# A retention and gated-MLP kernel on one core: the first heads' keys and values loaded unconverted and cast on three engines

## The chip, the cores and the metric

The kernel runs on one core of a Trainium2 chip. The metric is the device time of one launch in microseconds (us), the median of several runs. The engines of the core work side by side: TensorE (matmuls, PE in the profile, its weight loads PEld), VectorE (DVE), ScalarE (ACT), GpSimd (POOL) and SyncE (SP). Transfers are issued by SP, ACT and GpSimd and carried out by 16 DMA engines that all of them share. In the profile the loads that GpSimd issues are the queue q0, "software_dynamic"; those of SP and ACT are q1 and q10, "hardware_dynamic".

## The reference

Two layers follow each other, all in float32:

```python
# q, k, v: (8 batches, 8 heads, 576 positions, 64)
scores = q @ k.T / sqrt(64)
gamma  = 1 - 2 ** (-5 - head)
D      = gamma ** (i - j) where i >= j, else 0        # i query, j key position
ret    = (scores * D) @ v                             # (8, 8, 576, 64)
x      = ret with the heads side by side              # (4608, 512)
h      = x @ w_in                                     # (4608, 2048)
g      = h * clip(h + 3, 0, 6) / 6
out    = g @ w_out                                    # (4608, 512)
```

The inputs are q, k and v of 9.4 MB each and two weights of 4.2 MB each.

## The kernel before

**Tiles.** The 576 positions of a batch are cut into a head of 64 and a rest of 512. The heads of all eight batches together are one block of 512 tokens (block 0); the rests are blocks 1 to 8. Block 0 has a special path, in which the eight attention heads are taken in four pairs i = 0 to 3. The rests are worked in 36 chunks of 128 positions, with a running state between chunks. A block's result xT (512 features by 512 tokens) goes into the first product in 16 units ("up" units), each of eight matmuls that accumulate in PSUM, followed by one operation on ACT (u, L514) and one on DVE (g, L516), and then into the second product. From block 2 on that is a Strassen scheme with sums of weights and of g.

**Order.** Everything stands under a manual schedule: the order in which the program names operations is the order on each engine, and a queue that waits holds everything behind it on that engine. A hand-written plan (strings and tables) orders all that comes after block 0's first units. The changed lines lie ahead of this plan, in the first 25 us.

**Block 0 in the old order (L752 to L822).** `indices` and `make_identity` make small tables. Keys and q of pair 0 are loaded in float32 by SP and ACT (`load_half`, L403, one load for each head of the pair, 128 partitions of 1 KB); q of the other pairs follow on the same two queues. On GpSimd's queue come the keys of pairs 1 to 3 (six loads), the values of all pairs (eight loads, `load_values`, L443), the four pieces of w_in (`win_piece`, L679, the first in two halves) and the four of w_out (`wout_piece`, L684). All loads of this queue convert from float32 to float16 on the way. Loads with `keys` as last argument wait until the first keys have landed. Between the first two key loads and the rest GpSimd sets `pick` to zero (L767), a table of 128 x 2048 float16 that `picks` later fills with four strided copies of `by_chunk`.

`distances` (L107 to L113, on DVE) makes the table of i - j, with a huge number where j > i; `mask_of_heads(i)` (L118, on ACT) makes exp(log(gamma) x distance) for the two heads of a pair. For each pair, `cast_heads` makes float16 of keys or q (L416), `turn_heads` transposes them by eight small matmuls and a copy out of PSUM (L423, L428, L430), `scores_heads` forms the scores and multiplies them by the mask on DVE (L471, L474), `values_heads` brings the values into the order of the keys by 32 matmuls with `pick` and a copy (L454, L455), and `inner_heads` multiplies scores and values and copies the result into xT (L483, L485). `idle_products(n)` are matmuls whose result is not used. The first four up units are interleaved, one quarter of the accumulation at a time, because quarter i needs only the result of pair i.

Behind the up units, `decays` (16 small operations on GpSimd and one on ACT) makes the powers that the chunks need, `mask_of_chunk` and `decays_of_chunk` the mask and the powers of a chunk (GpSimd, L133 to L138 and L130). `fetch(8, wout[0])` lets SP load the first chunks, and waits for the first piece of w_out to land, so that these loads don't compete with the weights.

PSUM has six buffers of one kind (`pp`: scores, inner products, up units) and two of another (`st`: transposes and values).

```python
        if nm not in hd.setdefault(i, {}):
            if queue is nc.gpsimd:
                hd[i][nm] = heads16(i, nm)
```

These lines of `load_half` give GpSimd's loads a float16 target, and with it the conversion.

Of the kernel before, what the change touches and what calls it, by code (L numbers as in the profile page):

```python
# [21 lines left out]
def kernel(  # L22
# [9 lines left out]
    nc = tc.nc  # L32
# [356 lines left out]
    def after(i, behind):  # L389
        tc.add_manual_dep(i.ins, behind.ins.name,  # L390
                          mybir.DependencyInfo(mybir.DependencyClass.Sync, mybir.DependencyReason.SCHED_ONLY),
                          reason="goes first")

    def load_half(i, nm, e, queue, behind=None):

        if nm not in hd.setdefault(i, {}):
            if queue is nc.gpsimd:
                hd[i][nm] = heads16(i, nm)
            else:
                f = half_tile(io, "fq", i, FP32, "hq", bufs=2) if nm == "q" else io.tile(  # L400
                    [P, H * D], FP32, tag=f"f{nm}", name=f"h{nm}{i}")
                hd[i][nm] = f.rearrange("p (e j d) -> p e j d", e=2, j=NJ)
        d = queue.dma_start(hd[i][nm][:, e].rearrange("p j d -> p (j d)"),  # L403
                            dict(q=q, k=k, v=v)[nm][:, 2 * i + e, 0:TL, :].rearrange("b (r j) d -> r b (j d)", j=NJ))
        if behind is not None:
            after(d, behind)
        return d

    def heads16(i, nm):
        if nm == "q":  # L410
            return half_tile(work, "q16", i, FP16, "hq16_", bufs=2).rearrange("p (e j d) -> p e j d", e=2, j=NJ)
        return work.tile([P, 2, NJ, D], FP16, tag=f"{nm}16", bufs=dict(k=4, v=NV16)[nm], name=f"h{nm}16_{i}")
# [22 lines left out]
    def picks():  # L435
        for j in range(NJ):
            nc.vector.tensor_copy(pick[:, j].rearrange("p c (x j) -> p (c x) j", j=NJ)[:, :, j], by_chunk)

    def load_values(i, behind=None):

        t = heads16(i, "v")
        for e in range(2):
            d = nc.gpsimd.dma_start(t[:, e].rearrange("p j d -> p (j d)"),  # L443
                                    v[:, 2 * i + e, 0:TL, :].rearrange("b (r j) d -> r b (j d)", j=NJ))
            if behind is not None:
                after(d, behind)
        hd.setdefault(i, {})["v"] = t

    def values_heads(i, copy):

# [224 lines left out]
    def win_piece(n, parts=1, behind=None):  # L675
        a, b = pieces_in[n]
        for i in range(parts):
            cc = slice(NP // parts * i, NP // parts * (i + 1))
            d = nc.gpsimd.dma_start(win16[n][:, cc], win_v[:, cc, BLK * a:BLK * b])  # L679
            if behind is not None:  # L680
                after(d, behind)

    def wout_piece(pc):
        return nc.gpsimd.dma_start(wout16[:, JQ * pc:JQ * pc + JQ, :], wout_v[pc])  # L684
# [63 lines left out]

    with tc.manual_schedule(engines={ENG.PE, ENG.DVE, ENG.Pool, ENG.Activation, ENG.SP}):
        sp, act, pool = nc.sync, nc.scalar, nc.gpsimd  # L750
        on_act, on_dve = nc.scalar.copy, nc.vector.tensor_copy
        indices()  # L752
        for nm in ("k", "q"):
            landed = load_half(0, nm, 0, sp)
            keys = landed if nm == "k" else keys
            load_half(0, nm, 1, act)
        nc.scalar.activation(warm, half, ACTF.Exp)
        load_half(1, "q", 0, sp)
        load_half(1, "q", 1, act)
        for i in (2, 3):  # L760
            for e in range(2):
                load_half(i, "q", e, sp, keys)
        for i in (1, 2, 3):
            for e in range(2):
                load_half(i, "k", e, pool, None if i == 1 else keys)
            if i == 1:
                nc.gpsimd.memset(pick, 0.0)  # L767
        for i in range(NP):
            load_values(i)
        win_piece(0, 2)  # L770
        for n in (1, 2, 3):
            win_piece(n)
        wout = [wout_piece(pc) for pc in (0, 2, 1, 3)]
        distances()
        idle_products(5)
        mask_of_heads(0)
        cast_heads(0, "k", on_dve)
        picks()
        turn_heads(0, "k", on_act)
        mask_of_heads(1)  # L780
        idle_products(4)
        cast_heads(0, "q", on_dve)
        mask_of_heads(2)
        turn_heads(0, "q", on_act)
        cast_heads(1, "q", on_dve)
        turn_heads(1, "k", on_act)
        turn_heads(1, "q", on_act)
        cast_heads(2, "q", on_dve)
        scores_heads(0)
        mask_of_heads(3)  # L790
        idle_products(1)
        turn_heads(2, "k", on_act)
        turn_heads(2, "q", on_act)
        cast_heads(3, "q", on_dve)
        scores_heads(1)
        idle_products(1)
        turn_heads(3, "k", on_act)
        turn_heads(3, "q", on_act)
        scores_heads(2)
        values_heads(0, on_act)  # L800
        scores_heads(3)
        values_heads(1, on_act)
        inner_heads(0, on_act)
        values_heads(2, on_dve)
        inner_heads(1, on_dve)
        values_heads(3, on_act)
        inner_heads(2, on_dve)
        first = [up_steps(0, u) for u in range(4)]
        for dmc in range(3):
            for unit in first:  # L810
                next(unit)
            if dmc == 1:
                inner_heads(3, on_act)
        for unit in first:
            for _ in unit:
                pass
        decays()
        mask_of_chunk()
        decays_of_chunk()
        fetch(8, wout[0])  # L820
        for u in range(4, NFC):
            up_unit(0, u)  # L822
        weight_sums(3)
# [74 lines left out]
```

## Time and profile before

| What | Value |
|---|---|
| Median of three runs | 299.42 us (298.52 to 299.57) |
| The profiled execution | 301.09 us, its span 299.4 us |
| Granted TensorE clock | 1.00 |
| Loaded through GpSimd's queue | 4720 packets, 5.11 MB written |
| Read from HBM, written to it | 36.70 MB, 9.44 MB |

The span runs from the first to the last recorded instruction; the execution's own time is 1.7 us longer. "Busy" counts work of an engine and not its waits. In a timeline each line has the start in the span, the length (of all the instructions that were merged into it), the engine, the line of the kernel, the operation with what it writes and reads, and how often; in brackets stands the idle time ahead of it and what ended it. A DMA instruction on an engine's line is only the issue; the transfer comes later.

### The profile page before, as it was taken

To read this page: it belongs to the slowest core of one execution; us is meant where nothing else is said; L and a number is where in the kernel's file an instruction comes from. 1 tells how busy PE (TensorE), PEld (TensorE's weight loads), DVE (VectorE), ACT (ScalarE), POOL (GpSimd) and SP (SyncE) were. 2 spreads that over 40 slices of the span, in tenths; PEclk is the share of its full clock that TensorE was granted. 3 is DMA by queue.
4 is the path that set the end of the run, shared out by engine and by line. 5 is a ranking of instruction groups with operands and counts; after the bars stand their busy time and mean duration, and the time that the engine had idled before them with its cause. 6 is when DMAs were issued, how large, how long until landed. Compare 5 with 4: busy or idle time off the path is not lost.

```text
span 299.4 us, 12624 instructions
## 1 busy us (share of the span) xinstructions
PE 287.2 (96%) x5574; PEld 219.8 (73%) x5574; DVE 216.0 (72%) x380; ACT 190.5 (64%) x343; POOL 133.9 (45%) x169
## 2 busy tenths in 40 slices
PE   4998999999999999999989999999999999999995
PEld 2675655877556667898768878988787787778894
DVE  8648768859835678788957796678759776647654
ACT  3738855778866687585767577667766574565420
POOL 8961046656841912529621962296237003100510
PEclk9999999999999999999999999999999999999999
DMA  7999989996999999999999899989908100200114
GB/s 164 148 182 214 231 204 228 242 243 120 186 209 168 246 197 221 172 202 205 239 219 212 147 201 215 151 162 259 141 11 145 73 2 29 102 15 2 72 72 140
DMA packets 119542, 47.86 MB, mean 160 GB/s; under 512 B 92352, under 2 KB 114880, under 8 KB 119488
## 3 DMA queue, kind: packets, MB, share of 16 engines
q1 hardware_dynamic: 114336, 41.56, 71.3%
q0 software_dynamic: 4720, 5.11, 10.6%
q8 instruction: 43, 0.70, 1.0%
q10 hardware_dynamic: 432, 0.39, 0.5%
q14 instruction: 11, 0.09, 0.1%
HBM read 36.70 MB, written 9.44 MB: 154 GB/s over the span
## 4 chain that ended last, share of the span: by engine, by line
PE 77%; DMA 10%; POOL 6%; ACT 3%; DVE 2%; issue 1%; SPq 0%; POOLq 0%; ACTq 0%
PE ph L153 36%; PE pm L153 29%; DMA wout<-in_moe_w_out_dram 5%; PE pd L153 4%; PE po L232 3%; DMA fq<-in_q_dram 3%; PE pa L232 2%; DMA fv<-in_v_dram 2%; POOL hv L443 1%; POOL hk L403 1%; POOL win L679 1%; PE pu L232 1%; POOL q L192 1%; ACT z L327 1%; ACT kT L211 1%
## 5 line engine op out<-in xcount | busy, mean ns | idle before, releaser
L153 PE MATMUL ph<-xT,win 128*64 128x512 f16 (+1 forms) x1248 | 144.5, 364 | 1.5 <-DMA win<-in_moe_w_in_dram 1.5
L516 DVE SCALAR_TENSOR_TENSOR g<-u,ph 128x512 f16<-128x512 f32 x132 | 89.6, 684 | 50.4 <-ACT u L514 49.9
L514 ACT ACTIVATE u<-ph,half 128x512 f32<-128x512 f32 x132 | 90.3, 691 | 42.6 <-PE ph L153 40.1
L153 PEld LDWEIGHTS <-win 128*64 128x64 f16 x1248 | 83.1, 136 | 28.4 <-DMA win<-in_moe_w_in_dram 2.1
L153 PEld LDWEIGHTS <-g 128*64 128x64 f16 x928 | 50.6, 110 | 15.5 <-issue 0.4
L153 PEld LDWEIGHTS <-s 128*64 128x64 f16 x896 | 51.0, 110 | 8.2 <-issue 1.1
L321 POOL TENSOR_TENSOR z<-z,gpow 128x256 f32<-128x256 f32 x24 | 16.2, 673 | 67.5 <-DVE z L320 44.8
L153 PE MATMUL pm<-ws,s 128*64 128x256 f16 x672 | 46.1, 273 | 0.2 <-issue 0.2
L192 POOL TENSOR_TENSOR q<-fq,dec 128x512 f16<-128x512 f32 x30 | 35.6, 1204 | 17.2 <-DMA fq<-in_q_dram 17.2
L195 POOL TENSOR_TENSOR v<-fv,dec 128x512 f16<-128x512 f32 x32 | 36.2, 1134 | 2.6 <-PE ph L153 2.6
L612 POOL TENSOR_TENSOR u<-u,p 128x512 f32<-128x512 f32 x7 | 8.9, 1271 | 62.0 <-ACT u L652 55.8
L373 ACT CAST xT<-po 128x256 f16<-128x256 f32 (+1 forms) x44 | 22.6, 585 | 21.4 <-PE po L232 21.4
L153 PE MATMUL pd<-wout,g 128*64 128x512 f16 x256 | 34.2, 382 | 0.1
L153 PE MATMUL pm<-wout,g 128*64 128x256 f16 x448 | 30.8, 273 | 0.0
L267 DVE TENSOR_TENSOR a<-pa,mask 128x256 f16<-128x256 f32 (+1 forms) x44 | 21.9, 539 | 10.3 <-PE pa L232 6.9
L548 DVE TENSOR_TENSOR s<-g 128x1024 f16<-128x1024 f16 x28 | 19.4, 694 | 0.2
L327 ACT CAST z<-z 128x512 f16<-128x512 f32 x24 | 14.9, 620 | 7.0 <-DVE z L317 6.6
L188 ACT CAST k<-fk 128x512 f16<-128x512 f32 x29 | 18.0, 621 | 1.0 <-DMA fk<-in_k_dram 1.0
L153 PE MATMUL pm<-ws,g 128*64 128x256 f16 x224 | 16.9, 274 | 0.0
L153 PE MATMUL pm<-wout,s 128*64 128x256 f16 x224 | 16.7, 273 | 0.2
L232 PE MATMUL po<-qT,z 64*64 64x64 f16 x512 | 12.6, 198 | 1.3 <-ACT z L327 0.7
L232 PEld LDWEIGHTS <-z 64*64 64x64 f16 x512 | 8.0, 106 | 7.5 <-ACT z L327 2.5
(111 smaller groups left out, 292.6 us busy)
## 6 DMA issues: line engine op xcount, KB each, us to landing
fk<-in_k_dram SPq DMA_DIRECT2D x32, 256.0 KB, 4.7
fq<-in_q_dram SPq DMA_DIRECT2D x16, 512.0 KB, 6.0
fv<-in_v_dram SPq DMA_DIRECT2D x32, 256.0 KB, 5.7
out_dram<-o SPq DMA_DIRECT2D x14, 512.0 KB, 3.6
wout<-in_moe_w_out_dram POOLq DMA_DIRECT2D x4, 512.0 KB, 18.9
out_dram<-o SPq DMA_DIRECT2D x7, 256.0 KB, 5.7
win<-in_moe_w_in_dram POOLq DMA_DIRECT2D x3, 512.0 KB, 12.5
hq<-in_q_dram SPq DMA_DIRECT2D x6, 128.0 KB, 4.7
```

Of the source, the lines that this page charges most:

```text
L153: nc.tensor.matmul(out[r], lhs[:, r], rhs, skip_group_check=True, **flags)
L188: (nc.gpsimd.tensor_copy if c in K_POOL else nc.scalar.copy)(by_head(k16), in_rows(st[c]["fk"]))
L192: (nc.vector if e and c in Q_DVE else nc.gpsimd).tensor_tensor(by_head(q16[:, e]), in_rows(st[c]["fq"][:, :, e, :]), in_rows(dd[:, 2 + e, ...
L195: nc.gpsimd.tensor_tensor(v16, st[c]["fv"], dd[:, 1, H:2 * H, :], ALU.mult)
L232: return lambda: nc.tensor.matmul(*args, skip_group_check=True, **flags)
L267: nc.vector.tensor_tensor(a16[:, a, 0:n].rearrange("p x i q -> p (x i) q"), pa[a].rearrange("p x i q -> p (x i) q"), m, ALU.mult)
L321: nc.gpsimd.tensor_tensor(new, new, decay, ALU.mult)
L327: nc.scalar.copy(z16, zs[c])
L373: nc.scalar.copy(xt[:, s], po[s].rearrange("p x n (e r) -> p x n e r", e=2))
L514: nc.scalar.activation(uu[:, 0:n], ph[:, 0:n], ACTF.Relu, bias=half, scale=1.0 / 6.0)
L516: nc.vector.scalar_tensor_tensor(out=g[:, hf, ths, jr, :], in0=by_half(uu), scalar=1.0, in1=by_half(ph), op0=ALU.min, op1=ALU.mult)
L548: nc.vector.tensor_tensor(*pend.popleft())
```

## The change

- Keys and values of block 0 that GpSimd loads come as float32 into float32 tiles, on the same queue, and are cast on the way to their use: keys of pairs 1 to 3 on DVE, values of pair 0 on ACT, values of pairs 1 to 3 on GpSimd. `load_values` goes.
- `distances` and all four `mask_of_heads` come ahead of the rest of the heads' work.
- `mask_of_chunk` and `decays_of_chunk` move from behind the up units to GpSimd's place between the keys of pair 1 and the other loads, where the memset of `pick` was. That memset goes to DVE.
- GpSimd's loads come in another order (values 0, keys 2, keys 3, values 1 to 3), then pieces 0 and 1 of w_in, then GpSimd's three casts, then pieces 2 and 3 and w_out.
- The first scores come ahead of the transposes of pair 1's q; `picks` comes after them; values of pair 0 are worked before the scores of pair 2, and the first inner product before the scores of pair 3. Two copies move from DVE to ACT. Three idle products stand where four were.

```diff
-            if queue is nc.gpsimd:
-                hd[i][nm] = heads16(i, nm)
-            else:
-                f = half_tile(io, "fq", i, FP32, "hq", bufs=2) if nm == "q" else io.tile(
-                    [P, H * D], FP32, tag=f"f{nm}", name=f"h{nm}{i}")
-                hd[i][nm] = f.rearrange("p (e j d) -> p e j d", e=2, j=NJ)
+            f = half_tile(io, "fq", i, FP32, "hq", bufs=2) if nm == "q" else io.tile(
+                [P, H * D], FP32, tag=f"f{nm}", name=f"h{nm}{i}")
+            hd[i][nm] = f.rearrange("p (e j d) -> p e j d", e=2, j=NJ)
...
-        for i in (1, 2, 3):
+        distances()
+        for i in range(NP):
+            mask_of_heads(i)
+        for e in range(2):
+            load_half(1, "k", e, pool)
+        mask_of_chunk()
+        decays_of_chunk()
+        for i, nm in ((0, "v"), (2, "k"), (3, "k"), (1, "v"), (2, "v"), (3, "v")):
             for e in range(2):
-                load_half(i, "k", e, pool, None if i == 1 else keys)
-            if i == 1:
-                nc.gpsimd.memset(pick, 0.0)
-        for i in range(NP):
-            load_values(i)
+                load_half(i, nm, e, pool, keys)
         win_piece(0, 2)
-        for n in (1, 2, 3):
-            win_piece(n)
-        wout = [wout_piece(pc) for pc in (0, 2, 1, 3)]
-        distances()
+        win_piece(1)
         idle_products(5)
-        mask_of_heads(0)
         cast_heads(0, "k", on_dve)
-        picks()
+        nc.vector.memset(pick, 0.0)
         turn_heads(0, "k", on_act)
-        mask_of_heads(1)
-        idle_products(4)
+        idle_products(3)
         cast_heads(0, "q", on_dve)
-        mask_of_heads(2)
         turn_heads(0, "q", on_act)
-        cast_heads(1, "q", on_dve)
+        cast_heads(1, "k", on_dve)
         turn_heads(1, "k", on_act)
+        cast_heads(1, "q", on_dve)
+        scores_heads(0)
+        idle_products(1)
         turn_heads(1, "q", on_act)
+        picks()
+        cast_heads(0, "v", on_act)
+        cast_heads(2, "k", on_dve)
         cast_heads(2, "q", on_dve)
-        scores_heads(0)
-        mask_of_heads(3)
-        idle_products(1)
+        scores_heads(1)
         turn_heads(2, "k", on_act)
         turn_heads(2, "q", on_act)
+        idle_products(1)
+        values_heads(0, on_act)
+        cast_heads(3, "k", on_dve)
         cast_heads(3, "q", on_dve)
-        scores_heads(1)
+        scores_heads(2)
         idle_products(1)
         turn_heads(3, "k", on_act)
         turn_heads(3, "q", on_act)
-        scores_heads(2)
-        values_heads(0, on_act)
+        for i in (1, 2, 3):
+            cast_heads(i, "v", on_pool)
+        for n in (2, 3):
+            win_piece(n)
+        wout = [wout_piece(pc) for pc in (0, 2, 1, 3)]
+        inner_heads(0, on_act)
+        values_heads(1, on_act)
         scores_heads(3)
-        values_heads(1, on_act)
-        inner_heads(0, on_act)
-        values_heads(2, on_dve)
-        inner_heads(1, on_dve)
+        values_heads(2, on_act)
+        inner_heads(1, on_act)
         values_heads(3, on_act)
         inner_heads(2, on_dve)
...
         decays()
-        mask_of_chunk()
-        decays_of_chunk()
         fetch(8, wout[0])
```

More of the change, by code (lines that the diff above doesn't have):

```diff
@@ L437, in picks @@
             nc.vector.tensor_copy(pick[:, j].rearrange("p c (x j) -> p (c x) j", j=NJ)[:, :, j], by_chunk)
[L439 to L447, printed above, removed]
     def values_heads(i, copy):
@@ L750 @@
         sp, act, pool = nc.sync, nc.scalar, nc.gpsimd
-        on_act, on_dve = nc.scalar.copy, nc.vector.tensor_copy
+        on_act, on_dve, on_pool = nc.scalar.copy, nc.vector.tensor_copy, nc.gpsimd.tensor_copy
         indices()
@@ L762 @@
                 load_half(i, "q", e, sp, keys)
-        for i in (1, 2, 3):
-            for e in range(2):
-                load_half(i, "k", e, pool, None if i == 1 else keys)
-            if i == 1:
-                nc.gpsimd.memset(pick, 0.0)
-        for i in range(NP):
-            load_values(i)
+        distances()
[6 more added lines that the diff above has]
+        for i, nm in ((0, "v"), (2, "k"), (3, "k"), (1, "v"), (2, "v"), (3, "v")):
+            for e in range(2):
+                load_half(i, nm, e, pool, keys)
         win_piece(0, 2)
-        for n in (1, 2, 3):
-            win_piece(n)
-        wout = [wout_piece(pc) for pc in (0, 2, 1, 3)]
-        distances()
+        win_piece(1)
         idle_products(5)
-        mask_of_heads(0)
         cast_heads(0, "k", on_dve)
-        picks()
-        turn_heads(0, "k", on_act)
-        mask_of_heads(1)
-        idle_products(4)
-        cast_heads(0, "q", on_dve)
-        mask_of_heads(2)
-        turn_heads(0, "q", on_act)
-        cast_heads(1, "q", on_dve)
-        turn_heads(1, "k", on_act)
-        turn_heads(1, "q", on_act)
+        nc.vector.memset(pick, 0.0)
+        turn_heads(0, "k", on_act)
+        idle_products(3)
+        cast_heads(0, "q", on_dve)
+        turn_heads(0, "q", on_act)
+        cast_heads(1, "k", on_dve)
+        turn_heads(1, "k", on_act)
+        cast_heads(1, "q", on_dve)
+        scores_heads(0)
+        idle_products(1)
+        turn_heads(1, "q", on_act)
+        picks()
+        cast_heads(0, "v", on_act)
+        cast_heads(2, "k", on_dve)
         cast_heads(2, "q", on_dve)
-        scores_heads(0)
-        mask_of_heads(3)
-        idle_products(1)
+        scores_heads(1)
         turn_heads(2, "k", on_act)
         turn_heads(2, "q", on_act)
+        idle_products(1)
+        values_heads(0, on_act)
+        cast_heads(3, "k", on_dve)
         cast_heads(3, "q", on_dve)
-        scores_heads(1)
+        scores_heads(2)
         idle_products(1)
```

## The prediction

> **What bounds the kernel now.** I read the page's busy shares first, then the chain that ended last, then the waits of TensorE, then the first 45 us engine by engine, because the change touches nothing behind that. On the page TensorE is busy nearly all the time:
>
> ```profile
> PE 287.2 (96%) x5574; PEld 219.8 (73%) x5574; DVE 216.0 (72%) x380; ACT 190.5 (64%) x343; POOL 133.9 (45%) x169
> ```
>
> so only its start and its gaps can move. The chain in order of time (start, length, what) shows that the start isn't TensorE's own:
>
> ```profile
> 3.05 1.81 POOL ws L767
> 4.86 2.57 POOL hk L403 x4
> 7.43 3.10 POOL hv L443 x6
> 10.55 1.04 POOL hv L443 x2
> 11.59 3.61 POOL win L679 x5
> 15.20 15.97 DMA wout<-in_moe_w_out_dram
> ...
> 31.80 9.42 DMA fq<-in_q_dram
> ...
> 41.39 1.46 POOL q L192
> ...
> 42.89 0.64 PE ptq L153 x16
> ```
>
> GpSimd issues one long stream of loads, the DMA engines work it off, the first piece of wout lands at 31.17, the loads of the chunks are held back for it, and TensorE meets that chain at 42.89. The waits of TensorE from 16 to 45 us say how near its own work is:
>
> ```profile
> PE ph L153 <- DMA win<-in_moe_w_in_dram: 1.5, 2, 1.0
> PE ptq L153 <- POOL q L192: 0.2, 1, 0.2
> ```
>
> and its timeline where they are:
>
> ```profile
> 17.89 0.39 PE L483 MATMUL hpo<-ha,ws 128*64 128x128 f16 x8
> 18.77 1.95 PE L153 MATMUL ph<-xT,win 128*64 128x512 f16 x16 [0.49 <-DMA win<-in_moe_w_in_dram]
> ...
> 23.68 10.58 PE L153 MATMUL ph<-xT,win 128*64 128x512 f16 x96 [0.98 <-DMA win<-in_moe_w_in_dram]
> ```
>
> At 18.77 it waits for the first half of w_in's piece 0, at 23.68 for piece 1; from there it has no gap of 0.1 us until 42.89. So two things set the end: when piece 1 lands, and when wout's first piece lands. Both are the GpSimd stream. The heads' work on the other engines only has to be done by 22.7.
>
> **The stream itself.** Is it held by issue or by the DMA engines? The queues in the windows 7 to 9 and 9 to 11 us (packets, MB, share of the 16 engines):
>
> ```profile
> q0 software_dynamic: 337, 0.16, 60.9%
> q1 hardware_dynamic: 345, 0.31, 57.5%
> ...
> q0 software_dynamic: 634, 0.29, 118.3%
> ```
>
> Shares add to over 100%: the engines are full. A packet of the converting queue costs 1.183 x 16 x 2 us / 634 = 60 ns, one of the unconverted q loads 0.575 x 32 / 345 = 53 ns, though the first writes 512 B and the second 1 KB. Both read 1 KB. The packet records give medians of 60 and 47 ns for these, and 98 and 324 ns for converting packets that read 2 and 8 KB: a slope by bytes read, plus some 22 ns on GpSimd's queue against 9 on the others. Even the 4-byte completion packets take 22 against 9. I read the 13 ns as a cost of that queue, not of converting.
>
> **The change, part by part.**
> - Loads without conversion: 14 loads of 128 packets stay 14 loads of 128 packets that read 1 KB. Between 0 and 13 ns saved on 1792 packets, over 16 engines: 0 to 1.46 us of full DMA time; if the wider write costs anything, below nothing, which full-rate 1 KB writes on the other queue at 47 ns make unlikely. I take 0.
> - GpSimd before the stream: the memset of pick (1.84 us) goes; the mask and powers come (from 22.78 to 24.14 in the trace: 1.36). The stream starts 0.4 to 0.5 us earlier, at about 4.4; keys of pair 0 must have landed, which they had by 4.76 at the latest.
> - Twelve issues from 4.76 to 11.55 are 0.57 us each, and stay so: the first w_in issue moves to about 11.2. Its first packet came 1.75 us after its issue (13.30), just as for the first key load (1.75, then 3.5), and by then the last value packets were still in the engines. So issue and engines limit jointly, and of the 0.4 us I take 0.3.
> - Order: values of pair 0 are third, keys 2 and 3 one place later. By completion packets the k-th load is through at 6.0, 7.0, 8.0, 8.8, 9.3, 9.9, 10.4, 10.8, 11.2, 11.7, 12.4, 12.8, 13.2, 15.05 (one engine late, behind a 16 KB instruction fetch). So keys 1 land at 7.0, values 0 at 8.8, keys 2 at 9.9, keys 3 at 10.8, values 1 to 3 at 11.7, 12.8 and 15.1.
> - Three casts on GpSimd stand between piece 1 and piece 2. The row for this shape on GpSimd (L188) is 609 ns; under contention L195 shows 1.03 to 1.49. From 13.3: values 1 and 2 to 14.5, values 3 from 15.1 to 15.7. Behind them wait pieces 2 and 3, four wout loads, sixteen small operations and ACT's decays. Piece 2 is issued at 15.7 instead of 13.8. The engines need its descriptors when the fastest has done its 64 packets of pieces 0 and 1, from 13.3 at 79 ns a packet: 18.4. Issue plus 1.75 is 17.5. Hidden, with 0.9 us to spare; beyond that each us costs one. The decays end near 22.7, as before, ahead of ACT's turn at 24.4.
> - VectorE: three more casts (0.43 each), the memset of pick (unknown: between 0.06, its 128x1 memset, and GpSimd's 1.84; I take 0.7 by its 128x1024 f16 row, L548) and the picks later. The memset lies between the casts of k0 and q0, where VectorE waits for q anyhow. VectorE's distances sat blocked:
>
> ```profile
> 2.26 2.69 DVE L110 TENSOR_SCALAR early<-query,fj 128x128 f32<-128x128 f32 x1
> ```
>
> 0.2 us of work until GpSimd's memset was over (4.86). With it gone they end between 3.9 (right after the first two issues, 3.05) and 5.3 (after the mask, 4.4, plus the 0.87 that they took behind the memset); before it was 5.73. I take 4.4.
> - ACT: eight masks at once (steps of 0.30: 2.4 us), one cast and two more PSUM copies (0.48 steps, 0.59 long).
>
> I laid the heads' work out in the new order, each operation at the later of its engine being free and its operand, with the trace's steps (turn 0.43 cold, 0.27 warm; scores 0.54 and 0.32; values 0.91; masked scores on VectorE 0.61). For the old order this gives the third inner product at 17.70, where the trace has 17.89. New: first scores 7.9 (10.15 before), values of pair 0 at 12.2 (13.39), values of pair 3 at 17.2, third inner product 18.0, first up unit 18.2, all four done at 21.9 (22.7). ACT's extra 1.4 us eats most of the early lead, but TensorE still waits for the same two pieces. Gain of this part: nothing, hidden by the landing of piece 1; margin about 1.5 us, beyond which each us late costs one.
>
> **Sum.** Against the profiled execution's 301.09 us (span 299.4 and 1.7 around it): stream -0.3, everything else 0: 300.8. The median of the runs shown is 299.42, 1.67 below that execution, so 299.1. Half a per cent (1.5 us) is about what a measurement of this kernel can tell from no change: the three runs lie 1.05 apart.
>
> [...] The row: casts on VectorE ran beside GpSimd's issues. From 4.76 to 11.59, VectorE did four casts and most of the picks, some 2.5 us, and the twelve issues took 6.83 us against 12 x 0.53 (the shortest) = 6.4, so 0.4 us of delay at most. That is about a sixth of the copies' time, and for three more casts (1.3 us) it makes 0.2 us. [...]
>
> **Rivals.**
> 1. Faster: the 13 ns are the conversion's. Then the key and value packets are through up to 1.46 us earlier, and if unconverted issues are also shorter than 0.57 us the stream follows: -1.5 or a little more, 297.7. For it: 60 against 47 ns. Against: the 4-byte packets, and issue, which alone would allow 0.4. Chance 0.13.
> 2. Slower: VectorE and GpSimd shut each other out. GpSimd's issues queue behind VectorE's casts at full price instead of a sixth: three new casts of 0.43 and perhaps the memset (0.7) put the stream 1.3 to 2.0 us later, less the 0.3 gained: 300.4 to 301.1, and more if the mask operations are caught behind the distances too (0.9): 302.0. It decides as soon as w_in's first issue falls behind 11.6. For it: the 2.69 us row. Against: the issues above. Chance 0.17.
> 3. Slower: the heads are late. If the distances end at 5.7 and cold matmuls last to 13 us, unit 4 could go at 23.6; a landing of keys 1 at 9 instead of 7 adds 2. Then 300 to 301.5. Chance 0.10.
> 4. Slower: values 3 land late or casts run at 1.5 us; piece 2 is issued after 16.7 and the engines run dry. At 18.7 it costs 2 us: 301.4. Chance 0.05.
>
> The build shows the loads on GpSimd's queue in the type of the inputs, so the change does what it says.
>
> **The numbers.** Forecast, chance 0.55: 299.1, own range 298.3 to 300.0. The range of 297.8 to 301.2 takes in most of rivals 1 to 3. Faster by over 0.5%: rival 1 mostly (0.12) and the edge of the forecast (0.02): 0.14. Slower: rival 2 0.10, rival 3 0.06, rival 4 0.05, the forecast's edge 0.03: 0.24. Same: the remaining 0.62.
>
> **What would show it.** First scores near 8, first w_in issue near 11.2, software packets between 9 and 11 us at 60 ns (47: rival 1), VectorE's distances over by 4.4 to 5.3, GpSimd's third cast over by 16.7, unit 4 near 23.4 still released by w_in and wout's first piece landing near 30.9. The forecast is wrong if unit 4 is released by another engine than DMA, if the first w_in issue lies over 0.5 us from 11.2, or if time appears behind 60 us.

## The result, and the profile after

The changed kernel takes 303.42 us (median of four runs, 303.06 to 304.1), beside 299.5 us for the kernel before on the same chip: a ratio of 1.0129 (95% interval 1.0083 to 1.0175). A second measurement of both gave 303.51 us and 1.0138 (1.0101 to 1.0175). It is slower by 3.9 us; 299.1 was forecast, with a range up to 301.2. The profiled execution takes 304.1 us, its span is 302.3 us.

The page's busy shares say that no engine became the bound; TensorE is busy for 1.8 us more than before (287.2):

```profile
PE 289.0 (96%) x5574; PEld 225.4 (75%) x5574; DVE 215.3 (71%) x382; ACT 191.2 (63%) x346; POOL 134.2 (44%) x171
```

The chain in order of time (start, length, what) has changed its nature. Before, it ran through GpSimd's issues and the landing of wout, to 42.89. Now it starts with the landing of q 0 and from 8.49 us on is for the most part TensorE's own (87% of the span); late in it stands an "issue", time in which TensorE waited for nothing that the profile names:

```profile
1.58 6.26 DMA hq<-in_q_dram
...
14.24 1.75 PE hpv L153 x32
...
153.94 1.28 issue
```

TensorE's waits show the same two places: the start, and matmuls far behind the changed code (pm and po belong to blocks 1 to 8):

```profile
PE hptq L420 <- DVE hq L413: 2.1, 1, 2.1
...
PE pm L153 <- issue: 1.3, 2, 0.8
PE po L232 <- issue: 1.3, 1, 1.3
```

No wait for win is left. TensorE's timeline says why: the heads are done so late that w_in is there first.

```profile
8.49 0.64 PE L420 MATMUL hptq<-by_chunk,hq 128*64 128x128 f16 x8 [2.12 <-DVE hq L413]
...
9.80 0.61 PE L458 MATMUL hpa<-hqT,hkT 64*128 64x128 f16 x8 [0.25 <-ACT hqT L425]
...
14.06 1.92 PE L153 MATMUL hpv<-hv,ws 128*64 128x128 f16 x32
...
23.54 3.83 PE L153 MATMUL ph<-xT,win 128*64 128x512 f16 x33
```

The first scores start at 9.80, the values of pair 0 at 14.06 (13.39 before), the first up unit at 21.59 (18.77), and unit 4 follows at about 25.3 without a gap; before, it started at 23.68 and had waited 0.98 us for w_in. The 32 matmuls of values 0 take 1.92 us instead of 1.08, and a group of eight matmuls 0.64 instead of 0.39 to 0.41 until 16.5 us (10.9 before): TensorE runs at about half rate for 5.6 us longer. The page's row of the granted clock shows 9 throughout and doesn't tell this; the lengths do.

For the comparison of runs I use three numbers from the records of TensorE. **Front** is the start of matmul 330 of the work (about 30 us) against the profiled execution of the kernel before. **Rest** is how much more is lost or won from matmul 600 (about 44 us) to the last one. The third is the longest pause, from the start of one matmul to the start of the next, within four matmuls of **matmul 2652** of the code (about 140 us), where the changed kernel stands in both of its profiles. "Shift" says by how many matmuls added ahead the code of the rest lies further on.

| Kernel | Shift | Median, us | Ratio (95%) | First up unit | Front | Rest | 2652 |
|---|---|---|---|---|---|---|---|
| before | 0 | 299.5 | 1 | 18.77 | 0 | 0 | 0.11 |
| before, profiled again | 0 | one run | – | 18.55 | -1.33 | +0.27 | 0.11 |
| changed | 0 | 303.42 | 1.0129 (1.0083–1.0175) | 21.59 | +1.54 | +1.76 | 0.74 |
| changed, again | 0 | 303.51 | 1.0138 (1.0101–1.0175) | 20.10 | +0.05 | +2.13 | 1.46 |
| A converting | 0 | 300.16 | 1.0025 (1.0001–1.0049) | 19.60 | -0.45 | +0.93 | 0.11 |
| B old order, unconverted | 0 | 306.49 | 1.0220 (1.0179–1.0262) | 24.95 | +4.90 | +1.42 | 0.81 |
| C keys 1 held for q 0 | 0 | 305.38 | 1.0186 (1.014–1.0232) | 22.69 | +2.63 | +2.27 | 0.76 |
| D keys converting | 0 | 302.43 | 1.0107 (1.0071–1.0143) | 20.43 | +0.38 | +1.58 | 1.49 |
| E values converting | 0 | 301.83 | 1.0080 (1.0051–1.0109) | 20.77 | +0.72 | -0.31 | 0.21 |
| F 8 idle products | 10 | 301.23 | 1.0051 (1.0028–1.0074) | 20.94 | +0.89 | +0.55 | 0.21 |
| G full rate | 22 | 302.34 | 1.0111 (1.0063–1.0158) | 19.24 | -0.81 | +1.61 | 0.52 |
| H converting, full rate | 18 | 301.60 | 1.0065 (1.0035–1.0095) | 19.02 | -1.04 | +1.36 | 0.53 |
| I converting, 6 idle | 6 | 299.64 | 1.0007 (0.9982–1.0031) | 18.59 | -1.42 | +0.88 | 0.21 |
| J before, shifted | 22 | 301.68 | 1.0079 (1.005–1.0107) | 18.47 | -1.58 | +0.49 | 0.43 |
| K before, shifted | 10 | 301.15 | 1.0051 (1.0029–1.0073) | 18.63 | -0.15 | +1.01 | 0.27 |
| L changed, shifted | 22 | 303.47 | 1.0133 (1.0092–1.0173) | 20.86 | +0.81 | +0.15 | 0.77 |
| M before, late loads | 0 | 300.48 | 1.0054 (1.0031–1.0077) | 19.77 | -0.08 | -1.55 | 0.13 |
| N changed, 1 and 7 idle | 0 | 303.45 | 1.0147 (1.0125–1.017) | 20.57 | +0.51 | +2.35 | 0.76 |
| O converting, 1 and 7 idle | 0 | 298.82 | 0.9989 (0.9966–1.0013) | 18.77 | -0.69 | -0.47 | 0.11 |
| P as O, TensorE late | 0 | 302.10 | 1.0076 (1.0052–1.0101) | 22.01 | +1.96 | -1.81 | 0.13 |

In the two profiles of each kernel, the front is 1.46 us later on the average (+0.80 against -0.67) and the rest loses 1.8 us (+1.95 against +0.14). Between the two, from matmul 330 to 600, the changed kernel wins 0.6 us back, so 2.7 us are left between the profiled spans. The medians lie 3.9 us apart: both profiled executions of the kernel before were longer than its median (301.09 and 300.34 us against 299.5), and no trace shows the remaining 1.2 us. So I looked for two causes, one in the front and one in the rest.

### The profile page after: what moved, and what is told of

It reads as the page before. It is cut to its first block, busy times and chain, and to the rows that moved or that the text cites. A ratio compares the mean times of both kernels' runs of the same rounds, so it can differ in the third digit from the quotient of the medians.

```text
span 302.3 us, 12639 instructions
## 1 busy us (share of the span) xinstructions
PE 289.0 (96%) x5574; PEld 225.4 (75%) x5574; DVE 215.3 (71%) x382; ACT 191.2 (63%) x346; POOL 134.2 (44%) x171
## 4 chain that ended last, share of the span: by engine, by line
PE 87%; ACT 4%; DVE 3%; issue 2%; DMA 2%; POOL 1%; SPq 0%; ACTq 0%; DVEq 0%; POOLq 0%
PE ph L153 40%; PE pm L153 29%; PE pd L153 6%; PE po L232 3%; PE pa L232 2%; DMA hq<-in_q_dram 2%; PE hpv L153 2%; PE pu L232 1%; ACT z L327 1%; PE hpa L458 1%; DVE a L267 1%; ACT kT L211 1%; DVE g L503 1%; PE idle L153 1%; PE ptq L153 1%
## 5 line engine op out<-in xcount | busy, mean ns | idle before, releaser
L153 PEld LDWEIGHTS <-win 128*64 128x64 f16 x1248 | 86.5, 136 | 23.7
L153 PEld LDWEIGHTS <-g 128*64 128x64 f16 x928 | 51.9, 110 | 15.2 <-issue 1.2
L195 POOL TENSOR_TENSOR v<-fv,dec 128x512 f16<-128x512 f32 x32 | 35.5, 1112 | 2.1 <-DMA fv<-in_v_dram 2.1
L267 DVE TENSOR_TENSOR a<-pa,mask 128x256 f16<-128x256 f32 (+1 forms) x44 | 21.9, 540 | 10.5 <-PE pa L232 7.1
```

The costliest lines, as they stand in the source:

```text
L153: nc.tensor.matmul(out[r], lhs[:, r], rhs, skip_group_check=True, **flags)
L195: nc.gpsimd.tensor_tensor(v16, st[c]["fv"], dd[:, 1, H:2 * H, :], ALU.mult)
L267: nc.vector.tensor_tensor(a16[:, a, 0:n].rearrange("p x i q -> p (x i) q"), pa[a].rearrange("p x i q -> p (x i) q"), m, ALU.mult)
```

## Experiments: which part of the change costs

**A.** The changed kernel with `load_half` as it was (GpSimd's loads convert) and without the casts of keys and values.

```diff
-            f = half_tile(...) if nm == "q" else io.tile(...)
+            if queue is nc.gpsimd:
+                hd[i][nm] = heads16(i, nm)
+            else: ...
-        cast_heads(1, "k", on_dve)        # and k 2, k 3, v 0 to v 3
```

> The changed kernel with one part undone: keys and values are converted on the way again, without casts; order, masks and the memset on VectorE stay as changed. Theory A (the loads): unconverted loads travel in 4 KB packets, the q loads on the other queues take turns with them and land at 7.84 instead of 6.9 at the latest; so here q of pair 0 is cast before 7.0, the first scores stand near 8.5, matmuls reach their full rate by 11, unit 4 waits for w_in again at 23 to 23.7, and the ratio to the kernel before is 1.000 to 1.004. Theory B (the order): the new order is itself too long, so unit 4 comes at 25 or later, and the ratio stays at 1.010 or above.

300.16 us. The new order with its masks, memsets and issues costs 0.25%; the unconverted loads with their casts, all the rest.

**B.** The other part alone: the old order, loads unconverted (but for values 3, for room), casts of keys on VectorE, of values 0 on ACT, of values 1 and 2 on GpSimd.

> The kernel before with unconverted loads in the old order (values of pair 3 stay converted, because their float32 buffer is not free there), casts of keys on VectorE, of values 0 on ScalarE, of values 1 and 2 on GpSimd between piece 1 and 2 of w_in. Theory A: q of pair 0 is cast at 7.5 or later, the first scores come at 10.7 to 11.5 (10.15 before), unit 4 at 24.3 or later, and the ratio to the kernel before is 1.003 to 1.008. Theory B: q at 6.9 as before, unit 4 near 23.7, ratio 1.000 within 0.002.

306.49 us. In the old order the unconverted loads with their casts cost 7 us; TensorE waits for the casts of keys:

```profile
PE hptk L423 <- DVE hk L416: 5.3, 4, 2.0
```

The new order therefore softens what loads and casts cost, compared with casts put into the old one at these places; it isn't the loss.

**D and E.** The changed kernel with only keys, or only values, converting again.

> The changed kernel with its keys converted on the way, without their casts; the values stay unconverted with their casts. Theory A: only keys 1 are in flight while q of pair 0 is loaded, so q lands by 6.5 to 6.9 and most of the loss goes: ratio 1.003 to 1.007, unit 4 at 23.2 to 24. A theory by which GpSimd's casts, the late issue of pieces 2 and 3, or the values' packets cost the time keeps the ratio at 1.011 or above.

> The reverse: keys unconverted with their casts, values converted on the way without theirs. Theory A: q of pair 0 lands at 7 to 7.9 as in the changed kernel, full rate after 14, ratio 1.009 to 1.014. The theory that blames casts of values and the order on GpSimd's queue: ratio 1.002 to 1.005.

302.43 and 301.83 us: either half undone takes back 1 to 1.6 us, both together (A) 3.3. Their rests differ: with unconverted values (D) TensorE stands 1.49 us near matmul 2652, with unconverted keys alone (E) it does not.

**C.** The changed kernel, in which GpSimd's first key loads also wait for SP's half of q 0.

```diff
-        for e in range(2):
-            load_half(1, "k", e, pool)
         mask_of_chunk()
         decays_of_chunk()
+        for e in range(2):
+            load_half(1, "k", e, pool, landed)
```

> The changed kernel, with GpSimd's first key loads (pair 1, unconverted) held until SP's half of q of pair 0 has landed, and its mask work ahead of them. Theory A (4 KB packets take turns with the q loads): q of pair 0 lands by 5.5 to 6 and is cast there, the first scores come at 8.0 to 8.6 although keys 1 land later (8), the matmuls' full rate is reached before 13, 1 to 2 us are won over the changed kernel (ratio to before 1.005 to 1.010). Theory B (order): nothing is won, or 0.5 to 1 us lost by the later stream.

305.38 us, worse. q 0 was cast at 6.00, where the changed kernel's two profiles have 7.94 and 6.79, so by this one profile the first software loads beside it do hold it back (in the kernel before, GpSimd's memset kept most of them away until 4.76); but the wait moved to keys 1:

```profile
PE hptk L420 <- DVE hk L413: 3.6, 2, 3.4
```

## Experiments: the rate of TensorE

**F.** 8 idle products ahead of the turn of q 0 instead of 3.

> The changed kernel with eight idle products where it has three, so that TensorE has work while it waits for q of pair 0; nothing else. Theory C (the clock): TensorE's matmuls ran at half their rate until 16.5 us because it idled from 6.4 to 8.5; with the wait filled they reach the full rate by 11, although q lands as late as before (7.8), unit 4 comes at 23.5 to 24 instead of 25.3, and 1.3 to 1.8 us are won over the changed kernel. Theory A gives a smaller gain, since the late q alone costs 1.9. Theory B gives none, or a loss of up to 0.4 where the added matmuls end after q has landed.

301.23 us. The turn of q 0, at 8.54 us, runs at full rate, and the rate is lost again:

```profile
8.54 0.41 PE L420 MATMUL hptq<-by_chunk,hq 128*64 128x128 f16 x8 [1.16 <-DVE hq L413]
...
9.63 0.40 PE L458 MATMUL hpa<-hqT,hkT 64*128 64x128 f16 x8 [0.34 <-ACT hqT L425]
...
11.27 0.40 PE L458 MATMUL hpa<-hqT,hkT 64*128 64x128 f16 x8 [0.68 <-ACT hqT L425]
12.36 0.41 PE L420 MATMUL hptk<-by_chunk,hk 128*64 128x128 f16 x8 [0.69 <-DVE hk L413]
...
13.45 1.92 PE L153 MATMUL hpv<-hv,ws 128*64 128x128 f16 x32
```

Between 8.54 and 13.0 TensorE is never idle for more than 0.69 us at a time, yet values 0 run at half rate. The trace shows the fall behind three pauses of 0.34, 0.68 and 0.69 us within 3.1 us. The clock granted in the stretches of 3.3 us on both sides of the fall goes from 1.00 to 0.50 (the stretch, its length, busy time of PE, PEld, DVE, ACT and POOL, granted clock, DMA share, GB/s):

```profile
9.50:12.80 3.30, 1.80 (x38) 1.25 (x39) 2.68 (x9) 1.67 (x4) 2.47 (x4) 1.00 0.95 288
12.90:16.20 3.30, 3.30 (x52) 2.52 (x48) 1.96 (x5) 1.57 (x3) 3.26 (x6) 0.50 0.77 134
```

TensorE was busy for 1.80 of the 3.30 us ahead of the fall. How little is too little isn't settled: with 2.27 us (O, 9.6 to 12.9) the rate held, but in I it held with 1.69 (5.7 to 9.0) as well.

**G, H, I.** The pauses filled: in G the changed kernel with 8 products and three more on either side of `scores_heads(1)`; in H the same with converting loads and 6; in I converting loads with 6 and nothing in the pauses.

```diff
-        idle_products(3)
+        idle_products(8)
...
+        idle_products(3)
         scores_heads(1)
+        idle_products(3)
```

> The changed kernel with 8 idle products ahead of the turn of q 0 (3 before) and 3 more on either side of the scores of pair 1, the two places where TensorE stood 0.7 us and its rate fell back when only the first 8 were added (301.23). Theory 'a late q 0 and gaps keep TensorE at half rate': the turns (8 matmuls) take 0.39 to 0.41 us from 8.5 us on without falling back, the values of pair 0 take 1.08 instead of 1.92 us, the first up unit starts near 19.7 (21.59 in the changed kernel, 20.94 with 8 products), and the median falls by about 1 us more, to 300.2. Rival 'the loss is the waits for landings and casts, the rate is only their sign': the rate holds, but the first up unit starts at 20.9 or later and the median stays at 301.2 or above.

> The changed kernel with its loads converting again and without their casts (300.16 by itself), with 6 idle products ahead of the turn of q 0 (3 before) and 3 more on either side of the scores of pair 1. Theory 'what the new order still loses is TensorE's rate': full rate from 8 us on, the values of pair 0 in 1.08 instead of 1.92 us, the first up unit near 18.5 (19.60 by itself), where it begins to wait for w_in as in the kernel before; median 299.3, at the kernel before or a little under it. Rival 'the front is hidden behind w_in and the rest is late waits for instructions': 300.2, as without the products.

> As the kernel with converting loads and the new order (300.16), with 6 idle products instead of 3 ahead of the turn of q 0 and nothing else. Theory of the rate: full rate comes at about 7 us and falls back at 11 to 12.5 in the gaps of 0.7 us around the scores of pair 1, so a part of the gain: first up unit near 19.2, median 299.8. Rival: no change, 300.2.

The rate does as the theory says: in G every group runs at full rate from 8.07 us on, values 0 take 1.08 us, and the front is 0.81 us ahead of the kernel before's. The time does not: G stays 1.1% slower, and H, with a front 1.04 us ahead, is slower than the same kernel without the products (ratio 1.0065 against 1.0025, A). So the front is not the whole loss, and added matmuls cost something elsewhere. I (299.64) is level with the kernel before.

## Experiments: the rest

The pauses named "issue" follow the transfers of a queue of their own. The page of the changed kernel has it:

```profile
q8 instruction: 43, 0.70, 1.0%
```

These are 43 packets of 16 KB, one for some 130 of the 5574 matmuls with their weight loads, most of them 0.9 to 1.6 us long. By the queue's name and this count I take them for the fetches of TensorE's code; what is in them no run shows. Leaving out TensorE's waits for ScalarE, the 20 profiles have 58 pauses of over 0.4 us from 44 us on, at only ten places of the code: matmuls 735, 863 and 989, and within two of 1245, 2396, 2652, 2907, 3292, 3546 and 4441, which lie multiples of some 128 apart (the count takes in idle and added matmuls). The profile names 55 of them "issue". In all 58, TensorE goes on 1.22 to 1.61 us after the newest fetch was through. That it stands where it gets to the end of what is fetched before the next fetch is through and those 1.2 to 1.6 us are over is my reading of these times; the traces don't show it directly.

**J, K, L.** Does the place of the code matter by itself? 22 or 10 short matmuls (32 columns) are added where TensorE waits anyhow: in the kernel before, ahead of the turn of keys 0 (J, K); in the changed one, ahead of the turn of q 0 (L).

```diff
+    def short_products(n):
+        idle = psum.tile([P, NP, P], FP32, tag="pp", name="idle")
+        for _ in range(n):
+            product(idle[:, 0, 0:32], ident16, ident16[:, 0:32], start=True, stop=True)
...
         idle_products(5)
+        short_products(11)
```

> The kernel before with 11 short products (22 matmuls of 32 columns on the identity) more where TensorE waits 1.94 us for keys 0, so that the work stays in its order and every later instruction lies 22 matmuls further on in the code, as in the two kernels with products around the scores of pair 1. Theory 'the late waits hang on where the 16 KB instruction fetches fall': the front stays (first up unit near 18.8, waiting for w_in), the waits named issue behind 60 us change places, near matmul 3524 and 2376 by the work's count, and the median moves by 1 to 2 us, to 300.5 to 301.5. Rival 'the late waits come with the new order's traffic': the median stays within 0.5 us of the kernel before.

> As the kernel before with 22 short matmuls, with 10 of them, so that the code lies 10 matmuls further on, as in the changed kernel with 8 idle products ahead of q 0. Theory of the code's place: a median other than that of the kernel before by 0.5 to 1.5 us, in either direction, and other places of the late waits than with 22. Rival: within 0.5 us.

> The changed kernel with 11 short products (22 matmuls of 32 columns) ahead of the turn of q 0, where TensorE waits 2.1 us. Theory of the code's place: the late waits leave matmuls 2652, 2907 and 3546 and the median moves by over 0.7 us from 303.5; down to about 302, since the short products also bring full rate somewhat earlier. Rival 'the late waits come with the new order's traffic': the same sum of late waits behind 60 us (1.3 to 1.7 us over the kernel before), and 303 to 303.5.

It does. With the front no later than before (-1.58 and -0.15), the shift costs the kernel before 0.79% and 0.51%. The pauses leave their place in the work, as expected: K stands near matmuls 3534 and 4429 of the work for 1.25 and 1.37 us, as F does with the same shift (1.10 and 1.40), and no longer near 2905 (1.21 before). Counted in the code, with the ten added, these are 3544 and 4439, two of the ten places; the changed kernel stands near 3546 too, for 1.10 us. TensorE's waits between 100 and 240 us, of the kernel before, then of K:

```profile
PE po L232 <- issue: 1.0, 1, 1.0
PE pm L153 <- issue: 0.2, 1, 0.2
```

```profile
PE pm L153 <- issue: 1.2, 1, 1.2
PE ph L153 <- issue: 0.9, 1, 0.9
```

At the same place of the code the changed loads lose less: F and K are both at 1.0051, L against J is 0.54% (1.0133 against 1.0079), G against J 0.3%. The changed kernel shifted by 22 (L) did not get faster as a whole, 303.47; my expectation of 302 was wrong. The profiles don't show where J loses: its profiled execution (301.48) is about as long as the kernel before's (301.09), whose median is 2 us lower, so that cost rests on the medians.

**M.** Does a late front bring the late pauses, at the same place of the code? The kernel before with its memset of `pick` done twice.

> The kernel before with the memset of pick on GpSimd done twice: its loads, VectorE's distances and so TensorE's front come 1.84 us later; TensorE's code is the same to the instruction. Theory 'a later front alone brings other late waits': the front is 1.5 to 1.9 us later, the waits named issue appear near matmuls 2652, 2907 and 3546 as in the changed kernel, and the median is 303 or more. Rival 'the late waits are those of the changed loads, casts and order': the front's 1.5 to 1.9 us and no more, 301.0 to 301.4.

300.48 us. It did not test what it was meant to: the loads came later together with TensorE, and the front ended level (-0.08). Its profiled execution (299.77) was the quickest of ten.

**N and O.** The same eight idle products as in the changed kernel, but 1 at the start and 7 ahead of the turn of q 0, so that no instruction lies elsewhere: N with the changed loads, O with converting ones.

```diff
-        idle_products(5)
+        idle_products(1)
...
-        idle_products(3)
+        idle_products(7)
```

> The changed kernel with the same 8 idle products in other places: 1 at the start and 7 ahead of the turn of q 0 (5 and 3 before), so that TensorE works up to q 0 and no instruction lies elsewhere in the code. The kernel with 8 products more than that took 301.23 and the kernel before with its code shifted as far 301.15, so at that place of the code the changed loads cost nothing once the front is early. Theory 'place of the code and front are all': first up unit near 20.9 instead of 21.6, late waits as in the kernel before, 300 to 300.8. Rival 'late waits of its own at this place': 302 to 303, with the waits near matmuls 2652 and 3546 still there.

> As the kernel with converting loads and the new order (300.16), with 1 idle product at the start and 7 ahead of the turn of q 0: same code places as the kernel before, earlier full rate. By the theory of place and front: first up unit near 18.6 (19.60), TensorE then waits for w_in as in the kernel before; 299.2 to 299.6, level with it. Rival: 300.2, as without.

This pair tells most: 303.45 against 298.82 us, with the same order and code places, and the turn of q 0 at the same time (7.92 and 7.83). The first lines are N's, the second O's:

```profile
11.96 0.41 PE L420 MATMUL hptk<-by_chunk,hk 128*64 128x128 f16 x8 [0.69 <-DVE hk L413]
...
13.05 1.92 PE L153 MATMUL hpv<-hv,ws 128*64 128x128 f16 x32
```

```profile
11.30 0.41 PE L423 MATMUL hptk<-by_chunk,hk 128*64 128x128 f16 x8
...
12.54 1.06 PE L153 MATMUL hpv<-hv,ws 128*64 128x128 f16 x32
```

In N, TensorE waits 0.69 us for the cast of keys 2, which stands on VectorE behind the picks and the masked scores. That pause is one too many: in the 3.3 us ahead of the fall TensorE is busy for 1.80 us, as in F. Values 0 take 0.86 us longer, and the first up unit is 1.8 us later (20.57 against 18.77), of which 1.2 are left at matmul 330, since O waits for w_in there (0.4 us). That is the front's price of the casts. And N's rest is 2.8 us worse. The waits between 100 and 200 us, of N, then of O:

```profile
PE pm L153 <- issue: 2.0, 3, 0.9
```

```profile
PE po L232 <- issue: 1.2, 1, 1.2
```

**P.** O with two memsets more on VectorE ahead of the cast of q 2, which delay TensorE while its code and the loads stay as in O.

```diff
+        nc.vector.memset(ws[1].rearrange("p j n -> p (j n)"), 0.0)   # twice
         cast_heads(2, "q", on_dve)
```

> The kernel with converting loads, the new order and 1 and 7 idle products (298.82), with two memsets more on VectorE (0.91 us each, of a tile that is written again later) ahead of the cast of q 2: TensorE's front comes 1.8 us later or somewhat more, with its rate back at half in the gap, while the loads and TensorE's code stay as they are. First up unit near 20.6 to 21.3 (18.77 without), as in the two executions of the changed kernel (20.10 and 21.59). Theory 'late waits come of a front that is late against the loads, whatever the loads are': waits named issue near matmuls 2652 and 3546 appear, and the median is 302 or more. Rival 'they belong to the unconverted loads': the front's delay less what TensorE waited for w_in (0.35 us), 300.2 to 301, and no wait near 2652 and 3546.

TensorE waited 2.7 us for q 2 and fell to half rate (0.61 to 0.64 us for the groups of eight that start between 16.1 and 17.6 us, 0.39 to 0.42 for those ahead of the wait); the first up unit came at 22.01, later than in the changed kernel.

```profile
14.03 0.41 PE L423 MATMUL hptq<-by_chunk,hq 128*64 128x128 f16 x8 [2.71 <-DVE hq L416]
...
16.13 0.61 PE L461 MATMUL hpa<-hqT,hkT 64*128 64x128 f16 x8
```

302.10 us. O and P ran on different chips; by their ratios to the kernel before, P is 0.87% or 2.6 us slower, for a front that is 2.65 us later than O's. No pause came near 2652 or 3546 (0.13 and 0.21 us); the profile lists no wait of TensorE between 100 and 240 us. But the profiled execution was the quickest of six (300.84), so it may have missed some. In this one profile, a late TensorE alone doesn't bring the changed kernel's late pauses.

What goes with them is the unconverted values. Of the 13 profiles without a shift, the six with unconverted values (changed twice, B, C, D, N) stand 0.74 to 1.49 us near matmul 2652 and lose 1.4 to 2.4 us in the rest; the seven others (before twice, A, E, M, O, P) stand at most 0.21 us there, and their rest lies between -1.8 and +0.9. The fetch behind this place isn't slower there, it starts later: in the six, TensorE is at matmul 2636 to 2644 when it starts, in the seven at 2556 to 2570, but in P at 2615, so P came near to standing. With the code shifted the tie is looser: F has unconverted values and doesn't stand there (0.21), H and J have converting loads and stand 0.53 and 0.43 us. Why loads that are over by 16 us delay a fetch at 140 us is open. The code has one lead, which was not tried: the float32 tiles of keys and values take their turns in the same rotating buffers (tags fk and fv) as the chunks' loads, so that later chunks lie in other buffers than before.

No version beats the kernel before by more than the measurement tells: O (0.9989, 0.9966 to 1.0013) and I (1.0007) are level with it.

## Why the prediction was wrong

**"Sum ... everything else 0"** failed at both ends. It put the heads' work at nothing, "hidden by the landing of piece 1": the front came 1.46 us later, and nothing waited for piece 1. And nothing in it stood for work behind 60 us, where 1.8 us went (in the first profiles, 1.7 us of it are pauses named "issue" behind late fetches); the prediction had named time there as what would prove it wrong.

**The layout of the heads' work** failed in three terms. First scores at 7.9 need q 0 cast near 5.9 (the cast came 1.96 us ahead of the scores in the second profile). It came at 7.94 and 6.79, and at 6.48 and 7.18 in A and O with converting loads. In the kernel before it followed the picks at 6.90 without a wait: that row bounds the landing only from above, and I read it as hidden. In that kernel's second profile q 0 was cast at 7.32, after a wait for its landing. So the late q 0 isn't new: the early scores were a gain that neither order shows. Second, keys 2 were laid in at their landing, without their place on VectorE: 0.69 us (N). Third, the trace's cold and warm steps were used as if warm came at 11 us as before; with fewer products and a pause of 2.1 us it came at 16.5 (14.8 in the second profile).

**The margin** was right as a rule, but too wide. It said 1.5 us, "beyond which each us late costs one", and stood on one profile, in which unit 4 waited 0.98 us for w_in. In the kernel before's second profile it doesn't: TensorE waits for w_in once, for 0.77 us, ahead of the first up unit, and unit 4 starts at 22.34.

```profile
18.55 1.95 PE L153 MATMUL ph<-xT,win 128*64 128x512 f16 x16 [0.77 <-DMA win<-in_moe_w_in_dram]
20.33 0.39 PE L483 MATMUL hpo<-ha,ws 128*64 128x128 f16 x8
20.56 9.78 PE L153 MATMUL ph<-xT,win 128*64 128x512 f16 x88
```

The changed kernel starts unit 4 at 25.27 and 23.78, with no wait for w_in: late in both profiles by that measure. So rival 3 (the heads late, cold matmuls) named the right mechanism, given 0.10, though its conditions didn't come (the distances were early, at 3.44); its 300 to 301.5 has the front's size and lacks the late pauses.

**"The stream itself"** was half right. GpSimd's loads alone, in the window 10.5 to 12.5 us, before and then after (packets, MB written, share):

```profile
q0 software_dynamic: 592, 0.27, 114.4%
```

```profile
q0 software_dynamic: 234, 0.64, 99.0%
```

Converting packets read twice what they write, so that is 0.54 against 0.64 MB in 2 us, 270 against 320 GB/s: conversion does cost, and rival 1 had a point. But it bought nothing, since TensorE no longer waited for the stream. Of the 234 packets 155 carry 4 KB (194 ns each, the median), the others are the small ones of completion: here the rows of 1 KB are joined four to a packet, where the converting loads took one packet a row (60 ns). The prediction had the loads keep their 128 packets; they have 32. And the completion packets, its sign that the 13 ns are the queue's own, take 12 ns in this window instead of 22. Whether the larger packets hold back the q loads beside them can't be told: in the new order q 0 was cast between 6.48 and 7.59 with converting loads (A, H, I, O, P) and between 6.79 and 8.02 with unconverted ones (changed twice, F, G, L, N), which overlap.

**Issues and casts.** GpSimd after (start, length, what; in brackets the idle time ahead):

```profile
7.69 2.15 POOL L400 DMA_DIRECT2D hv<-in_v_dram  x3
10.12 0.52 POOL L400 DMA_DIRECT2D hv<-in_v_dram  x1 [0.28 <-DMA hv<-in_v_dram]
...
11.67 1.14 POOL L400 DMA_DIRECT2D hv<-in_v_dram  x1 [0.15 <-issue]
12.80 2.40 POOL L666 DMA_DIRECT2D win<-in_moe_w_in_dram  x3
15.25 1.73 POOL L413 CAST hv<-hv 128x512 f16<-128x512 f32 x3
```

The first w_in issue came at 12.80, not 11.2: the last value issues stood 0.78 us in three pauses, one of them named as a landing of values, and three issues took longer than the 0.57 laid in (0.83 and 1.00 of the three from 7.69 on, 1.14 at 11.67). The casts took 0.6 us each and the third was over at 16.98 (16.7 was the limit given). Both were hidden as forecast, because nothing waited for w_in or wout any more.

**VectorE** did better than forecast: the distances took 0.28 us instead of 2.69 and ended at 3.44 (4.4 taken), so GpSimd's memset had indeed blocked them; the memset of pick took 0.91 us (0.7 taken).

**Issues beside VectorE's work, and rival 2.** Issues beside VectorE's memset took 0.53 and 0.54 us. But the three long ones (from 7.69, 8.20 and 11.67) stand beside VectorE's casts (7.94 to 9.11) and its picks and casts (11.70 to 13.03), and N and O have one issue each of 1.28 and 1.21 us beside the picks. So rival 2's sign (first w_in issue behind 11.6) came, and up to 1.4 of its 1.6 us may be rival 2's own; no run separates them from the other delays. It cost nothing, because nothing waited for w_in.

## What to carry to other kernels

Price moved work by the pauses that it makes on TensorE, the rate included: here one cast that stood 0.69 us too late moved the first up unit by 1.8 us, and a queue made faster by 18% bought nothing. Where an operation follows another without a wait, the trace bounds its operand's landing from above only; take a second profile, and look at the packets, before counting on it as early. And compare kernels at equal places of the code: ten added matmuls cost this one half a per cent, as much as many an edit is worth.

## What the runs showed of the hardware

- TensorE fell back to half rate behind several short pauses (0.34, 0.68 and 0.69 us within 3.1 us in F, the granted clock 0.50 behind them), and also behind a long one (2.71 us in P); with the pauses filled by idle products it stayed at full rate (G and H: values 0 in 1.08 us, beside 1.92 in F).
- The queue "instruction" brought 43 packets of 16 KB; behind a late one TensorE stood for 0.4 to 1.5 us and went on 1.2 to 1.6 us after the packet was through, at places fixed in the code (58 pauses in 20 profiles, ten places).
- GpSimd's unconverted 1 KB rows travelled four to a packet (194 ns), the converting ones alone (60 ns); by itself, between 10.5 and 12.5 us, GpSimd's queue read 320 GB/s unconverted against 270 converting.
